# Fillers counted from TensorE's real idle time, a scheduler that tracks fetched instructions, and a new table of keys

## The chip, the cores and the metric

The kernel runs on one core of a Trainium2 chip. The number that counts is the device time of one execution in microseconds (us), as the median of several runs. TensorE (PE) does matrix products, VectorE (DVE), ScalarE (ACT) and GpSimd (POOL) do the element-wise work, and SyncE (SP) issues every transfer to and from the main memory. PE is in-order as seen here: a product that waits holds up all that is written behind it.

## The reference

Eight batches of eight heads, 576 positions, head size 64. Attention with two masks is followed by a gated block whose gate mixes positions:

```python
scores = scale * np.matmul(q, k.transpose(0, 1, 3, 2))
mask_local = (rel >= 0) & (rel < 32)
mask_strided = (rel >= 0) & (pos[None, :] % 32 == pos[:, None] % 32)
# heads 0..3 local, heads 4..7 strided; softmax; times v  -> x (8, 576, 512)
h = np.maximum(x @ w_in, 0.0)
u, v = h[..., :512], h[..., 512:]
v_n = (v - mean(v)) / np.sqrt(var(v) + 1e-06)
v_s = np.einsum('ts,bsd->btd', w_spatial, v_n) + b_spatial[None, :, None]
out = (u * v_s) @ w_out
```

`w_in` and `w_out` arrive as 64-bit floats, the rest as 32-bit floats.

## The kernel before

**The work.** A unit `t` of attention is a batch and a pair of heads; of the four units of a batch two are local and two strided. A unit loads q, k and v, computes scores (`f_s`: L412 local, 36 products; L522 strided, 32 products), masks and normalises them, transposes them on VectorE (L465, L572), copies them into `ptl` or `pts` on ScalarE and GpSimd (L342, L344), multiplies by v (`f_v`: L494 local, 6 products in each of two halves; L589 strided, 32 products), and rounds the result into a high and a low part (`x`, L364 and L352). These products use small pieces of the array and are called tiled.

The dense products are written as three products of high and low parts each. Per batch: `v` (L780, 16 groups of three, plus a tail tile), whose result passes `chain` (L742 to L767: relu, mean and variance, a power on GpSimd, the scaling) into `vn`; `u` (L822); `spatial` (L902, closed by two tail products L914 and L915, times `u` in L924); and `project` (L944), stored as `outT`. Each 64-bit weight tile is loaded raw (`weight`, staged in `vn`, `u` and `g`), converted by four VectorE or ScalarE steps (L654 to L676), and split into high (L342 or L344) and low part (L352).

An f32 product of the tiled kinds and of the fillers shows as two matmul records in the profile: 10 fillers in the order are x20 in the trace.

**What sets the order.** Nothing is written in the order in which it runs. `Program.add` collects operations with a key (a due time), the engines that may do them with a cost in ns, and what they read and write. `Program.order` then walks forward in modelled time, takes for the engine that is free first the ready operation with the smallest key, and fixes each engine's whole instruction list. `KEYS` shifts the keys: `a` for the first eight units of attention, `v` and `u` for the tiles of `w_in`, `o` for `w_out`, `s` and `t` for the spatial weights. When a dense operation comes up while PE is in tiled mode, `order` may put a ready tiled one with a key less than `near` later ahead of it.

**Fillers.** `emit` walks the fixed order again. Where PE would be idle by the model for over `WARM_GAP` before an operation with a `spare` region, it puts products with a tile of zeros (L1066) into that region, which the real product overwrites. Their number is the modelled gap divided by `WARM_COST` (double in the first 4 us). Operations with a spare are the scores, the products with v, and the first product of a `v` tile.

**Transfers.** SP issues all loads in one in-order list, so a load that waits for a buffer holds up those behind it. q, k and v have two buffers each. `cst`, the masks (L994), has the key -200. Score tiles `s` are a ring of two: a unit's scores wait until the masks of the tile that lay there before have been applied (L432, L537).

Of the kernel before, what the change touches and what calls it, by code (L numbers as in the profile page):

```python
# [21 lines left out]
P = 128  # L22
STRIDE = 32
# [9 lines left out]
SB = STRIDE // 4  # L33
# [5 lines left out]
KEYS = {  # L39
    "a": (-1894.0, -126.2, -779.7, -79.4, 376.7, -12.1, -10.1, 227.1,),  # L40
    "v": (-128.3, -81.4, -413.7, -1231.9,),
    "u": (-53.3, 26.9, 4.7, -65.3,),
    "s": (531.9, 556.2, 1682.3, 644.7,),
    "o": (302.1, 188.1, 252.3, 1053.5,),
    "t": (1077.7,),
    "lead": (2.85,),
    "dp": (1925,),
    "dpt": (159.07,),
    "fill": (-733.8, 1585.7, 207.5, -196.5, 2223.1, 42.9,),
    "near": (149.92,),  # L50
}
WARM_END, WARM_GAP, WARM_SLACK, WARM_COST = 110000.0, 300.0, 100.0, 165.0
DMA_RATE = 275.0
# [4 lines left out]
PE, ACT, DVE, POOL, DMA = "tensor", "scalar", "vector", "gpsimd", "sync"  # L58
# [67 lines left out]
class Program:  # L126
# [3 lines left out]
    def __init__(self):  # L130
        self.ops, self.writer, self.readers, self.spare = [], {}, {}, {}
        self.tiled, self.port = set(), {}

    def add(self, key, choices, fn, reads=(), writes=(), spare=None, tiled=False, port=()):

        n = len(self.ops)
# [4 lines left out]
        if tiled:  # L141
            self.tiled.add(n)
        deps = set()
# [19 lines left out]
    def order(self):  # L163
# [10 lines left out]
        taken = [False] * len(ops)  # L174
        mode = False
        issued = []
# [24 lines left out]
        while len(issued) < len(ops):  # L201
# [19 lines left out]
            n = heapq.heappop(ready[e])[1]  # L221
            if e == PE and mode and n not in self.tiled:
                near = [
                    op for op in ready[PE]
                    if op[1] in self.tiled and op[0] < ops[n][0] + KEYS["near"][0]
                ]
                if near:
                    heapq.heappush(ready[PE], (ops[n][0], n))
                    ready[PE].remove(min(near))
                    heapq.heapify(ready[PE])  # L230
                    n = min(near)[1]
# [30 lines left out]

    def emit(self, nc, warm):


        ends, free = {}, 0.0
        for at, n, e in self.order():
# [18 lines left out]
def attention_moe(ctx, tc, qT, kT, vl, vs, cst, w_in, w_out, wsp, wtail, out):  # L286
# [115 lines left out]
    def local_attention(t, due, q, kl, v, kin):  # L402
# [4 lines left out]
        def f_s(eng):  # L407
# [15 lines left out]
            due - 14, [(PE, 26 * 2 * S // STRIDE)], f_s, [(q,), *kin], [(p,) for p in s_ps],  # L423
            spare=(s_ps[0], lambda: s_ps[0]()[:32, :96]), tiled=True,
        )
# [61 lines left out]
        for c0 in (0, 3):  # L487
# [3 lines left out]
            def f_v(eng, c0=c0, o_ps=o_ps):  # L491
# [9 lines left out]
                due - 1.5, [(PE, 6 * 98)], f_v, [(v,), *ptok], [(o_ps,)],  # L501
                spare=(o_ps, lambda o_ps=o_ps: o_ps()[:32, :64]), tiled=True,
            )
# [5 lines left out]
    def strided_attention(t, due, q, k, v, kin):  # L509
# [8 lines left out]
        def f_s(eng):  # L518
# [13 lines left out]
            due - 14, [(PE, SB * 98)], f_s, [(q,), *kin], [(s_ps,)],  # L532
            spare=(s_ps, lambda: s_ps()[:32, :96]), tiled=True,
        )
# [49 lines left out]
        def f_v(eng):  # L584
# [12 lines left out]
        add(  # L597
            due - 1.5, [(PE, 4 * SB * 27)], f_v,
            [(v,), *(("pts", i) for i in range(4))], [(p,) for p in o_ps],
            spare=(o_ps[0], lambda: o_ps[0]()[:32, :64]), tiled=True,  # L600
        )
# [172 lines left out]
    def v_tile(key, step, x_at, m, toks):  # L774
        v_ps = r_pm.new()
        for kt in range(NT):

            def f(eng, kt=kt):
# [11 lines left out]
                toks(kt) + [("w_in", 1, kt, 0), ("w_in", 1, kt, 1)], [(v_ps,)],  # L790
                spare=None if kt else (v_ps, lambda v_ps=v_ps: v_ps()[:32, :128]),
            )
# [200 lines left out]

    add(-200, [(DMA, 330)], lambda eng: eng.dma_start(cst_sb, cst), (), [("cst",)])  # L994

# [66 lines left out]

    def warm(region, count):
        for _ in range(count):
            o = region()
            nc.tensor.matmul(  # L1066
                o, zeros, zeros[:, None, :].to_broadcast([P, o.shape[-1] // 32, 32]),
                start=True, stop=True,
            )
# [73 lines left out]
```

## Time and profile before

| | |
|---|---|
| median of three runs | 556.89 us (555.7 to 556.96) |
| the profiled execution's own time | 560.0 us |
| its span, first to last instruction | 557.7 us |
| PE busy (share of the span) | 526.0 us (94%) |
| DVE, ACT, POOL busy | 319.4, 234.1, 145.2 us |
| mean granted PE clock | 0.963 of full |
| transfers | 52.66 MB, 94 GB/s over the span |

All times in the prediction are on the span's axis, which starts at the first instruction. A row of a timeline gives start, duration (us), engine, line, operation, output<-input, shapes, count, and in brackets the idle time before it and what ended it; "issue" there means that nothing the profile shows was waited for. Records of one engine overlap by some 0.1 us, so a group's duration is from its first start to its last end. PEclk is the granted clock as a share of full speed.

### The profile page before, as it was taken

How to read it: one execution, taken by the hardware profiler on the slowest of the kernel's cores; microseconds unless marked ns; L12 is line 12 of the kernel's file. 1: busy time of each engine (PE TensorE's matmuls, PEld its weight loads, DVE VectorE, ACT ScalarE, POOL GpSimd, SP SyncE). 2: the span in 40 equal slices, each digit the busy share in tenths (PEclk: the TensorE clock that was granted, in tenths of full speed). 3: DMA queues.
4: the chain of work that ended last, by engine and by line, in shares of the span. 5: the costliest groups of instructions: out<-in, count | busy, mean ns of one | idle time of the engine just before them, and what ended most of it. 6: DMA issues, size and time to landing. Idle time of an engine off the chain costs nothing.

```text
span 557.7 us, 15920 instructions
## 1 busy us (share of the span) xinstructions
PE 526.0 (94%) x6608; PEld 486.5 (87%) x6608; DVE 319.4 (57%) x1010; ACT 234.1 (42%) x747; POOL 145.2 (26%) x235
## 2 busy tenths in 40 slices
PE   3687897999999999999999998999999999999997
PEld 2565795998989989999999987999899989998997
DVE  2856897725545377852974576862884462535232
ACT  3746655755665445331641444341642132313211
POOL 3544778645546132100310021200410010001000
PEclk8579887999999999999999999999999999999999
DMA  8735582315235232231251322231121200010011
GB/s 260 242 125 205 145 316 75 105 64 161 87 104 164 86 110 85 74 125 44 75 154 45 115 85 73 80 105 44 51 69 42 71 12 2 21 43 23 1 42 43
DMA packets 26103, 52.66 MB, mean 94 GB/s; under 512 B 3120, under 2 KB 11440, under 8 KB 26032
## 3 DMA queue, kind: packets, MB, share of 16 engines
q1 hardware_dynamic: 26032, 51.65, 29.1%
q8 instruction: 52, 0.85, 0.7%
q14 instruction: 19, 0.16, 0.1%
HBM read 42.21 MB, written 9.44 MB: 93 GB/s over the span
## 4 chain that ended last, share of the span: by engine, by line
PE 90%; DVE 3%; issue 2%; DMA 2%; SPq 1%; POOL 1%; ACT 1%; ACTq 0%; DVEq 0%
PE m L780 19%; PE m L944 19%; PE m L902 18%; PE m L822 17%; PE po L494 4%; PE po L589 3%; PE s L412 2%; PE s L522 2%; PE m L914 2%; DMA vn<-w_in 2%; PE m L915 2%; PE m L1066 1%; PE po L1066 1%; SPq L371 1%; PE s L1066 0%
## 5 line engine op out<-in xcount | busy, mean ns | idle before, releaser
L902 PE MATMUL m<-wsp_sb,vn 128*128 128x288 f32 x768 | 110.9, 295 | 0.0
L822 PE MATMUL m<-x,w_in_sb 128*128 128x288 f32 x768 | 108.0, 300 | 2.5 <-POOL w_in_sb L352 1.8
L822 PEld LDWEIGHTS m<-x,w_in_sb 128*128 128x128 f32 x768 | 105.2, 191 | 4.6 <-POOL w_in_sb L352 2.0
L944 PE MATMUL m<-g,w_out_sb 128*128 128x288 f32 x768 | 106.2, 297 | 0.0
L902 PEld LDWEIGHTS m<-wsp_sb,vn 128*128 128x128 f32 x768 | 105.3, 189 | 0.7
L944 PEld LDWEIGHTS m<-g,w_out_sb 128*128 128x128 f32 x768 | 103.4, 188 | 0.6
L780 PE MATMUL m<-w_in_sb,x 128*128 128x512 f32 (+1 forms) x408 | 103.3, 408 | 0.0
L780 PEld LDWEIGHTS m<-w_in_sb,x 128*128 128x128 f32 (+1 forms) x408 | 75.8, 190 | 20.4 <-issue 2.4
L760 POOL TENSOR_TENSOR bn<-bn,sel 128x1 f32<-128x1 f32 (+1 forms) x37 | 21.3, 576 | 215.4 <-DVE bn L755 212.4
L924 DVE TENSOR_TENSOR u<-m,u 128x288 f32<-128x288 f32 x64 | 28.3, 455 | 72.8 <-PE m L915 72.6
L364 ACT COPY o<-m 128x288 f32<-128x288 f32 x59 | 23.5, 399 | 104.6 <-PE m L944 91.8
L449 ACT ACTIVATE pl<-pl,ml 128x64 f32<-128x64 f32 (+1 forms) x160 | 53.6, 338 | 5.3 <-DVE ml L432 5.2
L747 DVE BATCH_NORM_STATS2 bn<-vv 128x6 f32<-128x512 f32 (+1 forms) x37 | 25.5, 689 | 53.0 <-ACT vv L742 52.8
L344 POOL TENSOR_SCALAR ptl<-pc 32x320 f32<-32x320 f32 (+3 forms) x80 | 31.6, 395 | 53.6 <-PE po L494 39.2
L836 ACT ACTIVATE u<-m 128x288 f32<-128x288 f32 x64 | 25.6, 408 | 38.2 <-PE m L822 36.5
L742 ACT ACTIVATE vv<-m 128x512 f32<-128x512 f32 (+1 forms) x37 | 22.1, 596 | 46.3 <-PE m L780 45.6
L364 ACT CAST x<-po 128x288 fp32r<-128x288 f32 x54 | 20.3, 399 | 50.0 <-PE po L494 25.7
L352 DVE TENSOR_TENSOR x<-po,x 128x288 fp32r<-128x288 f32 x64 | 27.2, 451 | 21.8 <-ACT x L364 21.4
L522 PE MATMUL s<-kbd,q 128*32 128x36 f32 x1024 | 13.3, 206 | 18.8 <-DVE ml L432 12.4
L767 DVE TENSOR_SCALAR vv<-vv,bn 128x512 f32<-128x512 f32 (+1 forms) x37 | 22.6, 614 | 14.0 <-POOL bn L760 13.9
L449 ACT ACTIVATION_READ_ACCUMULATOR pl<-pl,ml 128x1 f32 (+1 forms) x160 | 30.3, 189 | 0.0
L522 PEld LDWEIGHTS s<-kbd,q 128*32 128x32 f32 x1024 | 11.6, 115 | 20.5 <-issue 20.0
(116 smaller groups left out, 659.2 us busy)
## 6 DMA issues: line engine op xcount, KB each, us to landing
q<-qT SPq DMA_DIRECT2D x32, 295.0 KB, 4.4
outT<-o SPq DMA_DIRECT2D x64, 144.0 KB, 1.8
v_raw<-vs SPq DMA_DIRECT2D x16, 512.0 KB, 3.8
v_raw<-vl SPq DMA_DIRECT2D x16, 384.0 KB, 3.8
k<-kT SPq DMA_DIRECT2D x16, 304.0 KB, 4.6
kbd<-kT SPq DMA_DIRECT2D x32, 144.0 KB, 4.4
vn<-w_in SPq DMA_DIRECT2D x4, 512.0 KB, 7.6
x<-wsp SPq DMA_DIRECT2D x4, 288.0 KB, 5.7
```

The lines of the kernel that those rows point to most:

```text
L344: eng.tensor_scalar(dst(), src(), 1.0, 0.0, op0=ALU.mult, op1=ALU.add)
L352: eng.tensor_tensor(dst(), src(), f32(hi()), op=ALU.subtract)
L364: eng.copy(dst(), src())
L449: eng.activation(p_sb()[:m, u, :], p_sb()[:m, u, :], AF.Exp, bias=st()[:m, u : u + 1], scale=-1.0, accum_out=st()[:m, NU + u : NU + u + 1],)
L522: eng.matmul(s_ps()[STRIDE * i : STRIDE * i + STRIDE, 2 * RA * c : 2 * RA * (c + 1)].rearrange("p (j k) -> p j k", j=2), q()[:, r : r + ST ...
L747: lambda eng: eng.bn_stats(bn()[:m, 0:6], v()[:m]), [(v,)], [(bn,)],
L780: eng.matmul(v_ps()[:m, :], x_at(kt)[:, a, :], w_in_sb[:, w, kt, HF:], start=(kt == 0 and i == 0), stop=(kt == NT - 1 and i == 2),)
L822: eng.matmul(u_ps()[:, :HS], w_in_sb[:, w, kt, f * P : (f + 1) * P], xs[NHP * b + kt]()[:, a, r], start=(kt == 0 and i == 0), stop=(kt == ...
L836: lambda eng, u=u, f=f, u_ps=u_ps: eng.activation(u()[:, f * HS : (f + 1) * HS], u_ps()[:, :HS], AF.Relu),
L902: eng.matmul(s_ps()[:, :HS], vn()[:, a, kt, fs], wsp_sb[:, w, kt, r], start=(kt == 0 and i == 0), stop=False,)
L924: lambda eng, ug=ug, s_ps=s_ps: eng.tensor_tensor(ug(), s_ps()[:, :HS], ug(), op=ALU.mult),
L944: eng.matmul(o_ps()[:, :HS], w_out_sb[:, w, f, e * P : (e + 1) * P], g[a]()[:, f, :], start=(f == 0 and i == 0), stop=(f == NT - 1 and i = ...
```

## The change

Five edits go together.

1. Fillers: 256 columns wide in place of 64, 96 or 128; counted as half (`WARM_SHARE`) of the modelled gap divided by 427 ns, for gaps over 800 ns, and no longer ahead of `v` tiles in the order that results. The gap starts at `free`, the modelled end of PE's last operation. Before, where an operation had fillers, its own cost was overwritten by that of one filler before `free` was taken (the line `cost = WARM_COST ...`), so the next gap counted from too early; now the operation's own cost stands. By the orders, 74 fillers become 20.
2. The model of PE now keeps a stock of fetched products: it refills by one in 32 ns up to 200, each operation takes a number from it (72, 64 or 12 for the tiled ones, which is their count of records in the profile, 3 for others), and a shortfall costs 32 ns each. A tiled operation that is larger than the stock gives way to a ready dense one, and one may be put forward only if it is smaller than the stock.
3. Two costs in the model are raised: GpSimd's rounding copy (L344) and the strided product with v.
4. `cst` gets a key of its own, -952.3.
5. All keys are new. The sequence of the first eight units stays the same; among the weights, the second `u` tile (`u` entry 1) moves from eighth to third.

The diff, cut to its core:

```diff
 KEYS = {
-    "a": (-1894.0, -126.2, -779.7, -79.4, 376.7, -12.1, -10.1, 227.1,),
-    "v": (-128.3, -81.4, -413.7, -1231.9,),
-    "u": (-53.3, 26.9, 4.7, -65.3,),
-    "s": (531.9, 556.2, 1682.3, 644.7,),
...
+    "a": (-2171.5, -625.6, -893.2, -356.9, 1325.6, -222.2, -52.3, 22.3,),
+    "v": (-407.2, -245.7, -878.2, -1404.4,),
+    "u": (-86.3, -477.1, 14.3, -106.1,),
+    "s": (434.1, 1240.4, 3115.7, 449.8,),
...
+    "cst": (-952.3,),
+    "near": (280.07,),
 }
-WARM_END, WARM_GAP, WARM_SLACK, WARM_COST = 110000.0, 300.0, 100.0, 165.0
+WARM_END, WARM_GAP, WARM_COST, WARM_COLS, WARM_SHARE = 110000.0, 800.0, 427.0, 256, 0.5
+FETCHED, FETCH_COST = 200.0, 32.0
...
-            if e == PE and mode and n not in self.tiled:
-                near = [
-                    op for op in ready[PE]
-                    if op[1] in self.tiled and op[0] < ops[n][0] + KEYS["near"][0]
-                ]
-                if near:
+            if e == PE:
+                stock = min(FETCHED, stock + (now - since) / FETCH_COST)
+                since = now
+                other = []
+                if n in self.tiled:
+                    if self.tiled[n] > stock:
+                        other = [op for op in ready[PE] if op[1] not in self.tiled]
+                elif mode:
+                    other = [
+                        op for op in ready[PE]
+                        if self.tiled.get(op[1], FETCHED) < stock
+                        and op[0] < ops[n][0] + KEYS["near"][0]
+                    ]
+                if other:
...
                 mode = n in self.tiled
+                stock -= self.tiled.get(n, 3)
+                cost += FETCH_COST * max(0.0, -stock)
...
-                if n in self.spare:
-                    buf, region = self.spare[n]
-                    since = max([free, 600.0, *(ends[m] + 200.0 for m in buf.before)])
-                    if at - since > WARM_GAP and at < WARM_END:
-                        cost = WARM_COST if since > 4000.0 else 2.0 * WARM_COST
-                        warm(region, int((at - since - WARM_SLACK) / cost))
+                if n in self.spare and at < WARM_END:
+                    before = self.spare[n][0].before
+                    gap = at - max([free, 600.0, *(ends[m] + 200.0 for m in before)])
+                    if gap > WARM_GAP:
+                        found[n] = int(WARM_SHARE * gap / WARM_COST)
...
-        cost = {ACT: 95 + 0.833 * n, DVE: 70 + 0.52 * n, POOL: 110 + 0.95 * n}
+        cost = {ACT: 95 + 0.833 * n, DVE: 70 + 0.52 * n, POOL: 110 + 1.1 * n}
...
-            due - 1.5, [(PE, 4 * SB * 27)], f_v,
+            due - 1.5, [(PE, 4 * SB * 34)], f_v,
...
-    add(-200, [(DMA, 330)], lambda eng: eng.dma_start(cst_sb, cst), (), [("cst",)])
+    add(KEYS["cst"][0], [(DMA, 330)], lambda eng: eng.dma_start(cst_sb, cst), (), [("cst",)])
...
-    def warm(region, count):
+    def warm(buf, count):
         for _ in range(count):
-            o = region()
             nc.tensor.matmul(
-                o, zeros, zeros[:, None, :].to_broadcast([P, o.shape[-1] // 32, 32]),
+                buf()[:STRIDE, :WARM_COLS], zeros,
+                zeros[:, None, :].to_broadcast([P, WARM_COLS // STRIDE, STRIDE]),
                 start=True, stop=True,
             )
```

Lines of the changed kernel are 20 further down than those of the kernel before in the functions that matter here (L780 becomes L800, L432 becomes L452, L1066 becomes L1085). Three places show how the change moves instructions. The first is SP's list of loads at the start; q, k, `v_raw` and `kbd` (strided keys) belong to units of attention, `vn` is the staging tile of the first raw weights. Before:

```order
L371 DMA v_raw_117<-vl 128x768
L371 DMA vn_122<-w_in 128x1024
L371 DMA q_172<-qT 128x590
L371 DMA kbd<-kT 64x576 x2
L371 DMA v_raw_178<-vs 128x1024
L371 DMA vn_122<-w_in 128x1024
L994 DMA cst_sb<-cst 128x192
```

Now, from the same place:

```order
L391 DMA v_raw_117<-vl 128x768
L391 DMA vn_122<-w_in 128x1024
L1014 DMA cst_sb<-cst 128x192
L391 DMA q_167<-qT 128x590
L391 DMA kbd<-kT 64x576 x2
L391 DMA v_raw_175<-vs 128x1024
L391 DMA vn_122<-w_in 128x1024
```

The masks' load has moved ahead of one q, two halves of k, one v and the second weight tile. VectorE's list follows: the masking of the first scores (L452) now comes straight after the first step on the first weight tile, where before three more steps on weights stood between.

The second place is PE around the first products with v (`ptl`, tiles `po_388` and `po_414` before, `po_323` and `po_339` now) and the first `v` tile. Before:

```order
L522 MATMUL s_325<-kbd,q_247 32x36 x32
L1066 MATMUL po_388<-zeros 32x64 x16
L494 MATMUL po_388<-ptl,v_raw_117 64x96 x6
L1066 MATMUL po_414<-zeros 32x64
L494 MATMUL po_414<-ptl,v_raw_117 64x96 x6
L1066 MATMUL m_448<-zeros 32x128 x12
L780 MATMUL m_448<-w_in_sb,x_430 128x512 x3
L1066 MATMUL po_468<-zeros 32x64 x2
```

Now:

```order
L1085 MATMUL po_323<-zeros 32x256
L514 MATMUL po_323<-ptl,v_raw_117 64x96 x6
L514 MATMUL po_339<-ptl,v_raw_117 64x96 x6
L1085 MATMUL s_370<-zeros 32x256 x2
L542 MATMUL s_370<-kbd,q_312 32x36 x32
```

The 16 and the 12 fillers are gone, one of the new kind stands there, and the strided scores that stood ahead of the products with v come behind them. The first `v` products come later, behind the next local scores.

The third place is PE at those `v` products (`m_…` are their tiles) and the second local unit's product with v (`po_600`, `po_618` before, `po_571`, `po_582` now). Before:

```order
L1066 MATMUL m_555<-zeros 32x128 x4
L780 MATMUL m_555<-w_in_sb,x_430 128x512 x3
L1066 MATMUL m_570<-zeros 32x128 x2
L780 MATMUL m_570<-w_in_sb,x_430 128x512 x3
L1066 MATMUL m_581<-zeros 32x128 x2
L780 MATMUL m_581<-w_in_sb,x_430 128x512 x3
L1066 MATMUL po_600<-zeros 32x64 x7
L494 MATMUL po_600<-ptl,v_raw_438 64x96 x6
L1066 MATMUL po_618<-zeros 32x64 x2
L494 MATMUL po_618<-ptl,v_raw_438 64x96 x6
```

Now:

```order
L800 MATMUL m_533<-w_in_sb,x_354 128x512 x3
L800 MATMUL m_543<-w_in_sb,x_354 128x512 x3
L800 MATMUL m_558<-w_in_sb,x_354 128x512 x3
L514 MATMUL po_571<-ptl,v_raw_356 64x96 x6
L514 MATMUL po_582<-ptl,v_raw_356 64x96 x6
L800 MATMUL m_592<-w_in_sb,x_354 128x512 x3
L1085 MATMUL s_610<-zeros 32x256
L542 MATMUL s_610<-kbd,q_548 32x36 x32
```

The `v` products stand side by side with no fillers between, and one filler in place of 17 is left in this stretch.

More of the change, by code (lines that the diff above doesn't have):

```diff
@@ L131, in __init__, with add @@
         self.ops, self.writer, self.readers, self.spare = [], {}, {}, {}
-        self.tiled, self.port = set(), {}
-    def add(self, key, choices, fn, reads=(), writes=(), spare=None, tiled=False, port=()):
+        self.tiled, self.port = {}, {}
+    def add(self, key, choices, fn, reads=(), writes=(), spare=None, tiled=0, port=()):
         n = len(self.ops)
@@ L141, in add @@
         if tiled:
-            self.tiled.add(n)
+            self.tiled[n] = tiled
         deps = set()
@@ L174, in order @@
         taken = [False] * len(ops)
-        mode = False
+        mode, stock, since = False, FETCHED, 0.0
         issued = []
@@ L221, in order @@
             n = heapq.heappop(ready[e])[1]
-            if e == PE and mode and n not in self.tiled:
-                near = [
-                    op for op in ready[PE]
-                    if op[1] in self.tiled and op[0] < ops[n][0] + KEYS["near"][0]
-                ]
-                if near:
+            if e == PE:
[12 more added lines that the diff above has]
+                if other:
                     heapq.heappush(ready[PE], (ops[n][0], n))
-                    ready[PE].remove(min(near))
+                    ready[PE].remove(min(other))
                     heapq.heapify(ready[PE])
-                    n = min(near)[1]
+                    n = min(other)[1]
             cost = dict(ops[n][1])[e]
@@ L261, in order, with fillers @@
         return sorted(issued)
-    def emit(self, nc, warm):
-        ends, free = {}, 0.0
-        for at, n, e in self.order():
+    def fillers(self, issued):
+        ends, free, found = {}, 0.0, {}
+        for at, n, e in issued:
             cost = dict(self.ops[n][1])[e]
@@ L270, in emit @@
             if e == PE:
-                if n in self.spare:
-                    buf, region = self.spare[n]
-                    since = max([free, 600.0, *(ends[m] + 200.0 for m in buf.before)])
-                    if at - since > WARM_GAP and at < WARM_END:
-                        cost = WARM_COST if since > 4000.0 else 2.0 * WARM_COST
-                        warm(region, int((at - since - WARM_SLACK) / cost))
-                free = at + cost
+                if n in self.spare and at < WARM_END:
[3 more added lines that the diff above has]
+                        found[n] = int(WARM_SHARE * gap / WARM_COST)
+                free = at + cost
+        return found
+    def emit(self, nc, warm):
+        issued = self.order()
+        fillers = self.fillers(issued)
+        for _, n, e in issued:
+            if e == PE and fillers.get(n):
+                warm(self.spare[n][1], fillers[n])
             self.ops[n][2](getattr(nc, e))
@@ L423, in local_attention @@
             due - 14, [(PE, 26 * 2 * S // STRIDE)], f_s, [(q,), *kin], [(p,) for p in s_ps],
-            spare=(s_ps[0], lambda: s_ps[0]()[:32, :96]), tiled=True,
+            spare=(s_ps[0], s_ps[0]), tiled=72,
         )
@@ L501, in local_attention @@
                 due - 1.5, [(PE, 6 * 98)], f_v, [(v,), *ptok], [(o_ps,)],
-                spare=(o_ps, lambda o_ps=o_ps: o_ps()[:32, :64]), tiled=True,
+                spare=(o_ps, o_ps), tiled=12,
             )
@@ L532, in strided_attention @@
             due - 14, [(PE, SB * 98)], f_s, [(q,), *kin], [(s_ps,)],
-            spare=(s_ps, lambda: s_ps()[:32, :96]), tiled=True,
+            spare=(s_ps, s_ps), tiled=64,
         )
```

17 lines of the change are left out of this document (8 added, 9 removed).

## The prediction

> **What bounds the kernel now.** I read the busy times first, then the stretches, then PE's waits, then the start engine by engine.
>
> ```profile
> PE 526.0 (94%) x6608; PEld 486.5 (87%) x6608; DVE 319.4 (57%) x1010; ACT 234.1 (42%) x747; POOL 145.2 (26%) x235
> ```
>
> ```profile
> core 0: us, PE busy (x) PEld busy (x) DVE busy (x) ACT busy (x) POOL busy (x), PEclk, DMA share, GB/s
> 0.00:20.00 20.00, 7.95 (x196) 7.22 (x201) 8.27 (x34) 9.40 (x28) 6.54 (x17) 0.72 0.78 242
> 20.00:40.00 20.00, 15.63 (x324) 12.83 (x305) 12.12 (x44) 10.11 (x37) 12.31 (x20) 0.68 0.56 172
> 40.00:60.00 20.00, 16.39 (x273) 12.01 (x253) 14.15 (x45) 11.86 (x40) 8.37 (x8) 0.92 0.59 197
> 60.00:80.00 20.00, 18.19 (x238) 16.58 (x237) 18.38 (x38) 12.62 (x28) 15.36 (x18) 0.91 0.76 252
> 80.00:100.00 20.00, 17.12 (x219) 14.41 (x218) 15.94 (x43) 11.75 (x39) 16.41 (x16) 0.83 0.27 91
> ```
>
> PE is the bound, but in the first 100 us it is busy for only 75.3, and not all of that is work:
>
> ```profile
> sum 558.00, PE 20.23 PEld 15.92; mean PE 2.02 PEld 1.59
> ```
>
> That is the sum over the span for L1066 alone: 20.2 us are fillers. From 60 to 80 DVE is at 92%, so a front that comes sooner meets DVE next. PE's longest waits:
>
> ```profile
> PE s L522 <- DVE ml L432: 12.4, 2, 10.8
> PE s L522 <- issue: 6.4, 3, 3.4
> ```
>
> Idle time in sum is 557.7 - 526.0 = 31.7 us. So up to 52 us are not work, and nearly all of it lies in the start. What the change can win is there.
>
> **1. The masks' load (`cst`) earlier.** The 10.8 us are the wait of the first strided scores, which need a score tile back from the masks.
>
> ```profile
> 6.19 0.66 SPq L994 DMA_DIRECT2D cst_sb<-cst  x1
> ...
> DMA to landing us min/median/max: 8.8/8.8/8.8
> ...
> 9.88 0.43 DVE L661 TENSOR_SCALAR vn<-vn 128x512 int32<-128x512 int32 x1 [7.51 <-DMA vn<-w_in]
> ...
> 14.72 0.43 DVE L661 TENSOR_SCALAR vn<-vn 128x512 int32<-128x512 int32 x1 [2.70 <-DMA vn<-w_in]
> 15.08 0.23 DVE L432 CUSTOM_DVE_ANT_0 pl<-s,cst_sb 128x64 f32<-128x64 f32 x1
> ...
> 16.66 1.19 PE L522 MATMUL s<-kbd,q 128*32 128x36 f32 x64 [10.84 <-DVE ml L432]
> ```
>
> ```profile
> q<-qT SPq DMA_DIRECT2D x32, 295.0 KB, 4.4
> ...
> v_raw<-vs SPq DMA_DIRECT2D x16, 512.0 KB, 3.8
> ...
> kbd<-kT SPq DMA_DIRECT2D x32, 144.0 KB, 4.4
> vn<-w_in SPq DMA_DIRECT2D x4, 512.0 KB, 7.6
> ```
>
> `cst` landed at 6.19 + 8.8 = 15.0, and the masks began at once. Between the landings of the two `vn` tiles (9.88 and 14.72) came 295 + 2 x 144 + 512 + 512 = 1607 KB, 332 KB per us. Now `cst` (96 KB) stands behind the first `vn` and lands at 9.88 + 0.3 = 10.2; q and two `kbd` follow by 583/332 = 1.8 us, at 12.0. The ten masks took 15.08 to 16.6, so they end near 11.8, and the scores start at 12.0 in place of 16.66: **-4.6**. Lower bound of the gain 0.3 (if the second `vn`, which still lands at about 15, were what the chain waits for; VectorE has all masks written ahead of it, so I take the whole), upper 4.9 (15.08 to 10.2). The loads that `cst` is moved past come 0.3 us later, inside these numbers.
>
> **2. Fillers that overrun their gap.**
>
> ```profile
> 32.03 4.79 PE L1066 MATMUL m<-zeros 128*32 128x128 f32 x24
> ...
> 32.58 0.46 DVE L352 TENSOR_TENSOR x<-po,x 128x288 fp32r<-128x288 f32 x1 [0.98 <-ACT x L364]
> ...
> 36.76 0.96 PE L780 MATMUL m<-w_in_sb,x 128*128 128x512 f32 x3
> ```
>
> ```profile
> 40.25 2.22 ACT L342 COPY ptl<-pc 32x320 f32<-32x320 f32 x6
> ...
> 40.57 1.06 PE L1066 MATMUL m<-zeros 128*32 128x128 f32 x8
> ...
> 42.45 0.62 PE L1066 MATMUL m<-zeros 128*32 128x128 f32 x4
> 43.89 0.62 PE L1066 MATMUL m<-zeros 128*32 128x128 f32 x4
> 45.34 0.97 PE L1066 MATMUL po<-zeros 128*32 128x64 f32 x14
> 46.24 0.72 PE L494 MATMUL po<-ptl,v_raw 128*64 128x96 f32 x12
> ```
>
> The first `v` products had their last input at 32.58 + 0.46 = 33.04 and started at 36.76, 3.5 us after a start at 33.3. The products with v at 46.24 had `ptl` at 40.25 + 2.22 = 42.5; the four fills ahead of them take 1.06 + 0.62 + 0.62 + 0.97 = 3.3, the work between them 3 x 0.96, so without fills they start at 40.6 + 2.9 = 43.5: 2.7 us. Together **-6.2**.
>
> What replaces them: 12 fillers of 128 columns in 4.79 us are 0.40 each, in a stretch of half clock (below), so one of 256 columns is an estimated 0.80 there and 0.40 to 0.62 at full clock (two of 128 took 0.62 at 42.45). The six ahead of the second local scores last 4.8 us after 13.2, until 18; by the rate above that unit's k lands at about 17, and its masks stand on VectorE behind the first unit's transposition, which covers the last us. The six ahead of the third local scores stand behind a k that SP issues after a v load, which itself waits for a strided product; a v lands 3.8 us after its issue and the k after it, so cover is 4 to 5. The first four (3.2 us) end before the first q lands (4.4 after its issue). The other four (3.2 us) stand ahead of products whose inputs pass ScalarE and GpSimd first. I take 0; bounds 0 and +3.2 for those four, so the term lies between -3 and -8 (the latter if the other old fills, 20.2 - 4.8 - 3.3 = 12.1 us, overran by 15% too).
>
> **3. Instruction fetch.**
>
> ```profile
> 30.17 0.42 PE L494 MATMUL po<-ptl,v_raw 128*64 128x96 f32 x1 [2.83 <-issue]
> ...
> 55.32 0.32 PE L522 MATMUL s<-kbd,q 128*32 128x36 f32 x12 [3.43 <-issue]
> 55.58 8.80 PE L780 MATMUL m<-w_in_sb,x 128*128 128x512 f32 x30
> ...
> 319.66 7.16 PE L780 MATMUL m<-w_in_sb,x 128*128 128x512 f32 x30
> ```
>
> ```profile
> q8 instruction: 52, 0.85, 0.7%
> ```
>
> Both stalls fall inside a group that had started, so no input was missing. PE has 6608 products and as many weight loads; 52 instruction packets make one per 127 products. The stalls therefore look like a block that had not arrived, in stretches of heavy loads (the first three 20-us rows show DMA at 0.56 to 0.78). The second also cooled PE: the 30 products behind it took 8.80 us against 7.16. Cost 2.83 + 3.43 + 1.64 = 7.9. The change spaces tiled groups in the model and has 108 fewer records, which shifts every block edge. It has no term for loads, so I give it half: **-4**, bounds -7.9 and +3.4 (one more stall).
>
> [...]
>
> Later stalls in L522 are 6.4 - 3.43 = 3.0. The run strided product, two strided scores, local product occurs five times in a row of groups in both orders, so I change nothing: 0, bounds -3 and +3.
>
> **4. Spatial weights.** One tile of `wsp` now gets its low part on VectorE behind the scaling of the first tail tile (L787), before `spatial` can finish.
>
> ```profile
> 90.57 4.62 PE L780 MATMUL m<-w_in_sb,x 128*64 128x512 f32 x12
> 95.03 6.48 PE L902 MATMUL m<-wsp_sb,vn 128*128 128x288 f32 x48
> ...
> 97.97 1.51 DVE L767 TENSOR_SCALAR vv<-vv,bn 64x512 f32<-64x512 f32 x1 [0.17 <-POOL bn L760]
> ```
>
> The tail tile ended at 95.2 and was scaled by 99.5, 4.3 later; a low part (one element-wise step of that size, 1.5 by the same row) follows: 5.8. PE has 24 spatial products (half of 6.48, 3.2), a strided product of 64 records (1.19 by the row at 16.66, less at full clock) and local scores of 72 ahead, some 5. **+1**, bounds 0 and +3.
>
> Edits 3 and the keys otherwise only move work that lies beside PE; the amounts per engine are unchanged.
>
> **The sum and what VectorE allows.** -4.6 - 6.2 - 4 + 1 = -13.8. But VectorE must do the same steps before each PE group. Its setup is over before 4 us:
>
> ```profile
> 0.00:4.00 4.00, 3.06 (x20) 3.06 (x20) 1.25 (x5) 3.27 (x4) 3.30 (x14) 1.00 0.53 162
> ```
>
> Its first data come at 9.88; from there to 60 us it was busy 8.27 - 1.25 + 12.12 + 14.15 = 33.3 of 50.1 us. In 60 to 100, where it is pressed, its share is (18.38 + 15.94)/40 = 0.86. At that share 33.3 us take 38.8, and it comes forward by 11.3 us; at the 0.92 of 60 to 80 by 13.9. I take the first, since three engines hand work to each other in this stretch: **-11.3**. Against the span, 557.7 - 11.3 = 546.4. The profiled execution's own time is 560.0; the median of the runs, 556.89, lies 0.8 under the span. From the median, **545.6 us**.
>
> **The rivals.**
>
> *VectorE keeps pace at 0.92 and no stall is left.* For it: masks no longer queue behind weight steps. Against: GpSimd and VectorE slow each other when both are dense. -13.9 and up to -3 later: 540 to 543.
>
> *Only the masks' gain survives.* Late landings of v and q hold the next units where they were: SP's list is in order, and a v load waits for a product. -2 to -7: 550 to 555.
>
> *The front is lost again by 95 us.* `spatial` needs all the weight tiles; if VectorE's idle 16.8 us move elsewhere in place of going, it starts where it did: within 0.3%, which is about what a measurement of this kernel can tell from no change.
>
> *Slower: PE stays at half clock.* Fillers drop from 20.2 us to at most 20 x 0.80 = 16, and by count half the gap at full clock.
>
> ```profile
> 32.00:36.00 4.00, 4.00 (x21) 3.23 (x20) 3.31 (x5) 2.25 (x5) 2.34 (x2) 0.50 0.62 208
> 36.00:40.00 4.00, 4.00 (x118) 3.07 (x116) 0.39 (x2) 0.82 (x3) 2.07 (x6) 0.98 0.16 43
> ```
>
> Here full clock came after 4 us without a gap, which were mostly fillers, and each us of full-rate work costs one more at half. From 60 to 100 PE was busy 18.19 + 17.12 us; if over 11.3 us of that work run at half clock in their new place the gain is gone, at 15 the time is 561. That takes seven restarts at the 1.64 us of the one above. Against it: the clock from 60 to 80 was 0.91 although the 3.43 us stall had come shortly before.
>
> [...]
>
> **How the numbers follow.** Likeliest, 543 to 550: 0.50. Better than that: 0.17. Masks only: 0.13. Within 0.3%: 0.07. Slower: 0.13. Faster is 0.50 + 0.17 + 0.13 = 0.80. For 8 in 10, the range leaves out the slow case and the lowest edge: 537 to 556.
>
> **What would show it.** Right: first strided scores near 12 (term 1); no L1085 group directly ahead of a `v` product, and fewer than 16 us of L1085 (2); "issue" waits of PE under 7 us in all (3); the first spatial products near 84 rather than 95, with VectorE over 85% busy from 10 to 80 (sum). Wrong: PEclk at 0.5 between 45 and 80, new waits of PE on `w_in_sb` or on `ptl` in that stretch, or a new "issue" stall there.

## The result, and the profile after

The changed kernel takes 542.36 us (median of four runs, 539.54 to 543.93), the kernel before beside it 556.92 (555.70 to 557.15): a ratio of 0.9737, 95% interval 0.9691 to 0.9783. Forecast were 545.6, 537 to 556, and faster at 0.8. The profiled execution took 543.93 with a span of 542.1; that of before had 557.7, so the two traces differ by 15.6 us. In four later series the kernel before ran between 545.5 and 559.4 us (and once 831.93), most of the time near 551 or 555; a ratio leaves out runs more than 1.5% above the fastest, so differences of medians and ratios can differ by some us. The trace of before is of a long execution, 560.0 us, and there is one trace for each kernel: single traces show where time goes, and the medians of one series say how much.

Busy times after, and the first 100 us in five stretches (columns as in the prediction):

```profile
PE 515.1 (95%) x6500; PEld 471.4 (87%) x6500; DVE 323.9 (60%) x1026; ACT 235.5 (43%) x751; POOL 127.7 (24%) x215
```

```profile
0.00:20.00 20.00, 10.91 (x230) 5.82 (x230) 8.72 (x38) 9.91 (x30) 8.62 (x21) 0.83 0.87 267
20.00:40.00 20.00, 14.63 (x280) 9.38 (x278) 18.61 (x71) 16.38 (x59) 16.03 (x21) 0.91 0.79 225
40.00:60.00 20.00, 17.45 (x286) 14.70 (x287) 17.26 (x34) 12.55 (x35) 15.05 (x16) 1.00 0.82 254
60.00:80.00 20.00, 17.47 (x282) 14.50 (x281) 18.30 (x49) 14.59 (x43) 14.27 (x14) 0.91 0.55 187
80.00:100.00 20.00, 19.99 (x304) 19.25 (x297) 14.35 (x67) 17.00 (x70) 14.91 (x21) 1.00 0.43 133
```

DVE is now pressed from 20 us on (18.61, 17.26, 18.30 of 20), where before it had 12.12 and 14.15 in the second and third stretch. L1085 alone, over the span:

```profile
sum 543.00, PE 13.77 PEld 5.16; mean PE 13.77 PEld 5.16
```

So 13.8 us of fillers stand in place of 20.2. PE's waits, the longest first:

```profile
PE s L542 <- DMA kbd<-kT: 9.3, 2, 7.0
PE s L542 <- issue: 2.5, 2, 1.9
PE m L800 <- ACT u L856: 2.2, 1, 2.2
```

The 10.8 us for VectorE's masks are gone; the scores wait for the strided keys instead. The start (SP, VectorE, PE) and then PE up to the first `project` products, of which the last row has its counterpart of before beneath it:

```profile
2.57 0.43 SPq L1014 DMA_DIRECT2D cst_sb<-cst  x1
...
9.80 0.43 DVE L681 TENSOR_SCALAR vn<-vn 128x512 int32<-128x512 int32 x1 [7.43 <-DMA vn<-w_in]
10.28 0.22 DVE L452 CUSTOM_DVE_ANT_0 pl<-s,cst_sb 128x64 f32<-128x64 f32 x1
...
13.32 1.19 PE L542 MATMUL s<-kbd,q 128*32 128x36 f32 x64 [7.01 <-DMA kbd<-kT]
...
27.05 4.16 PE L1085 MATMUL s<-zeros 128*32 128x256 f32 x12
32.85 0.96 PE L432 MATMUL s<-k,q 64*32 64x64 f32 x72 [1.64 <-DMA k<-kT]
33.75 2.36 PE L800 MATMUL m<-w_in_sb,x 128*128 128x512 f32 x9
36.03 1.21 PE L514 MATMUL po<-ptl,v_raw 128*64 128x96 f32 x24
...
40.96 0.76 PE L542 MATMUL s<-kbd,q 128*32 128x36 f32 x64 [2.27 <-DMA kbd<-kT]
...
43.23 6.57 PE L800 MATMUL m<-w_in_sb,x 128*128 128x512 f32 x27
...
78.14 0.95 PE L922 MATMUL m<-wsp_sb,vn 128*128 128x288 f32 x6
...
90.13 6.69 PE L964 MATMUL m<-g,w_out_sb 128*128 128x288 f32 x48
```

```profile
106.88 6.69 PE L944 MATMUL m<-g,w_out_sb 128*128 128x288 f32 x48
```

At the first `project` product PE has done the same groups in both orders, so this row is the measure of the front in all that follows: 16.8 us sooner in these two traces. From there to the end it is 450.8 us before and 452.0 after. In the traces the change won in the front, all of it, and lost about 1 us behind it. How much an ordinary execution wins is less: one of 552 us with the same rest would start `project` near 99 (552 - 450.8, less the 2.3 us by which the profiled time exceeds its span; an estimate).

### The profile page after: what moved, and what is told of

Its sections match the earlier page's. It is cut to its first block, busy times and chain, and to the rows that moved or that the text cites. A ratio compares the mean times of both kernels' runs of the same rounds, so it can differ in the third digit from the quotient of the medians.

```text
span 542.1 us, 15698 instructions
## 1 busy us (share of the span) xinstructions
PE 515.1 (95%) x6500; PEld 471.4 (87%) x6500; DVE 323.9 (60%) x1026; ACT 235.5 (43%) x751; POOL 127.7 (24%) x215
## 4 chain that ended last, share of the span: by engine, by line
PE 83%; DVE 6%; DMA 4%; POOL 2%; issue 2%; SPq 1%; ACT 0%; POOLq 0%; ACTq 0%; DVEq 0%
PE m L964 19%; PE m L922 18%; PE m L800 17%; PE m L842 17%; PE po L609 3%; PE po L514 3%; DMA g<-w_in 2%; PE s L432 2%; PE m L934 2%; DMA kbd<-kT 2%; PE m L935 2%; PE s L542 2%; SPq L391 1%; POOL ptl L364 1%; DVE vv L787 1%
## 5 line engine op out<-in xcount | busy, mean ns | idle before, releaser
L800 PE MATMUL m<-w_in_sb,x 128*128 128x512 f32 (+1 forms) x408 | 100.9, 403 | 2.2 <-ACT u L856 2.2
L800 PEld LDWEIGHTS m<-w_in_sb,x 128*128 128x128 f32 (+1 forms) x408 | 74.8, 187 | 21.8 <-ACT u L856 2.4
L780 POOL TENSOR_TENSOR bn<-bn,sel 128x1 f32<-128x1 f32 (+1 forms) x37 | 21.4, 577 | 226.0 <-DVE bn L775 221.9
L767 DVE BATCH_NORM_STATS2 bn<-vv 128x6 f32<-128x512 f32 (+1 forms) x37 | 25.4, 687 | 42.0 <-ACT vv L762 41.9
L364 POOL TENSOR_SCALAR ptl<-pc 32x64 f32<-32x64 f32 (+3 forms) x83 | 32.9, 396 | 68.7 <-PE po L514 52.7
L362 ACT COPY ptl<-pc 32x64 f32<-32x64 f32 (+3 forms) x77 | 26.1, 339 | 6.9 <-DVE pc L485 3.9
L384 ACT CAST x<-po 128x288 fp32r<-128x288 f32 x49 | 18.5, 397 | 17.3 <-PE po L609 9.1
L372 DVE TENSOR_TENSOR g<-u,g 128x288 fp32r<-128x288 f32 x56 | 25.2, 460 | 1.1
```

Of the source, the lines that this page charges most:

```text
L362: eng.copy(dst(), src())
L364: eng.tensor_scalar(dst(), src(), 1.0, 0.0, op0=ALU.mult, op1=ALU.add)
L372: eng.tensor_tensor(dst(), src(), f32(hi()), op=ALU.subtract)
L384: eng.copy(dst(), src())
L800: eng.matmul(v_ps()[:m, :], x_at(kt)[:, a, :], w_in_sb[:, w, kt, HF:], start=(kt == 0 and i == 0), stop=(kt == NT - 1 and i == 2),)
```

## The experiments

This table has, beside the medians, two numbers of each profiled execution: the start of `project` (the front), and the time from there to the end of the span with the sum of PE's waits named "issue" of over 0.25 us in it.

| kernel | median us | ratio to before, 95% | project starts | rest of the span | issue waits in the rest |
|---|---|---|---|---|---|
| before | 552 to 557 | | 106.88 | 450.8 | 3.7 |
| after | 542.36 | 0.974 [0.969, 0.978] | 90.13 | 452.0 | 3.8 |
| a_again | 540.33 | 0.980 [0.976, 0.984] | 89.09 | 451.2 | 3.3 |
| b_cst5 | 555.89 | 1.005 [1.001, 1.008] | 103.33 | 448.6 | 2.4 |
| a_cst9 | 546.04 | 0.990 [0.986, 0.993] | 94.20 | 450.5 | 2.8 |
| b_newfill | 546.15 | 0.986 [0.980, 0.992] | 95.30 | 448.7 | 2.8 |
| b_nofill | 548.23 | 0.997 [0.994, 1.000] | 95.98 | 452.3 | 6.0 |
| b_shift | 548.04 | 0.989 [0.983, 0.995] | 97.53 | 450.5 | 2.3 |
| a_oldfill | 547.44 | 0.987 [0.978, 0.995] | 97.43 | 450.6 | 2.9 |
| a_nofill | 542.82 | 0.980 [0.974, 0.986] | 89.79 | 450.5 | 2.9 |
| a_narrow | 544.90 | 0.982 [0.976, 0.988] | 91.55 | 451.4 | 3.6 |
| c_k3 | 545.22 | 0.987 [0.981, 0.992] | 89.83 | 448.0 | 1.6 |
| c_front | 543.71 | 0.982 [0.978, 0.986] | 91.13 | 448.8 | 2.7 |
| c_front64 | 542.98 | 0.980 [0.976, 0.984] | 87.54 | 453.2 | 6.1 |

The names say the base: b for the kernel before, a for the changed one, c for further moves on the changed one. In some of them the lines stand a few further down. The changed kernel was run again beside `a_cst9`, `b_nofill` and `c_k3`, in one series with them:

> The changed kernel itself, once more, to stand beside the others of this series. Expected 540 to 544 us, and against the kernel before a ratio near 0.975 to 0.982. If the kernel before comes out near 551 in half of its runs again, as it did beside the first four experiments, the gain against those runs is 9 to 10 us and against the others (near 556) 14 to 15.

It came out at 540.33 (538.57 to 542.11, six runs), against 552.29 of before: 12.0 us, less than the 14.6 of the first series.

### The masks' load

`b_cst5` is the kernel before with SP's list alone changed.

```diff
+# SP's list only: the masks' load from 10th to 5th place
+moved = issued.pop(at)
+issued.insert(loads[3] + 1, moved)
```

> Before with the masks' load as fifth in SP's list in place of tenth, all else in its place (VectorE still has three weight steps ahead of the masks). Theory of the first term: masks at 12.0 (behind the weight steps that end there) in place of 15.1, first strided scores at 13.6, and 3 us of it kept to the end: 553 to 554.5. Rival, that the next landing of a weight tile (14.7, next in VectorE's list) holds the chain: 556 to 557.

Measured 555.89 against 552.07 of before in that series: not faster. (Its trace has `project` 3.6 us sooner than the long execution of before; the medians don't bear that out.) VectorE and PE at the start:

```profile
9.63 0.43 DVE L666 TENSOR_SCALAR vn<-vn 128x512 int32<-128x512 int32 x1 [7.26 <-DMA vn<-w_in]
...
15.28 0.43 DVE L666 TENSOR_SCALAR vn<-vn 128x512 int32<-128x512 int32 x1 [3.50 <-DMA vn<-w_in]
15.62 0.22 DVE L437 CUSTOM_DVE_ANT_0 pl<-s,cst_sb 128x64 f32<-128x64 f32 x1
...
17.20 1.19 PE L527 MATMUL s<-kbd,q 128*32 128x36 f32 x64 [11.38 <-DMA kbd<-kT]
```

The second weight tile's first step stands ahead of the masks in VectorE's list and waits for its load. The masks' data had landed at 10.1 us (issued at 2.58, 7.5 to landing) and lay there. `a_cst9` is the reverse: the order of the changed kernel, with the load put back behind the second weight tile.

```diff
+# SP's list only: the five loads behind it go ahead of the masks' load
+issued[at:at] = later
```

> The changed kernel with one move: the masks' load stands behind the second weight tile, as ninth of SP's loads, instead of fifth. VectorE's list keeps the masks straight behind the first weight step. Theory (the load and VectorE's place for the masks work only together, and the load then bounds the front): the load lands near 15, the masks start near 15, the first strided scores near 16.7 in place of 13.3, the first project product comes 3 to 4 us later, time 545 to 547. Rival (the front is bound by VectorE's later work, which has slack until 20 us to catch up): the scores are late by the same 3.4 us, but the first spatial products and project move by less than 1 us and the time stays at 541.5 to 543.5.

```profile
9.61 0.43 DVE L685 TENSOR_SCALAR vn<-vn 128x512 int32<-128x512 int32 x1 [7.23 <-DMA vn<-w_in]
15.14 0.23 DVE L456 CUSTOM_DVE_ANT_0 pl<-s,cst_sb 128x64 f32<-128x64 f32 x1 [5.11 <-DMA cst_sb<-cst]
...
16.73 1.19 PE L546 MATMUL s<-kbd,q 128*32 128x36 f32 x64 [10.83 <-DMA vn<-w_in]
```

Measured 546.04 against 540.33 of `a_again` in the same series: 5.7 us, and 5.1 at `project` (94.20 against 89.09). So the load is worth this where the masks also stand early in VectorE's list, and nothing where they don't. The early place alone, in the old order, was not run.

### The fillers

`b_newfill` has the order of before with the new fillers (10 of 256 columns in place of 74), `b_nofill` has none.

```diff
-                        warm(region, int((at - since - WARM_SLACK) / cost))
+                        pass
```

> The order of before, every instruction but the fillers in its place; the fillers alone by the new rule and width (10 of 256 columns in place of 74 narrow ones: 4, 1, 3 and 2 ahead of the first, second and fourth group and of the first v product). Theory that overrunning fillers were a term of their own: the 6.2 us of the prediction's second term go, less some clock lost in 36 to 50 us where nothing warms PE now: 550 to 553. Rival, that the order is what counted: 555 to 557, because the products then wait for VectorE in the same places.

> The kernel before without any fillers; order and everything else as before. Theory (the fillers only do harm where they overrun, and the clock they give is worth nothing while other engines bound the front): the same as the old order with the new, fewer fillers, 545 to 548 us, although the granted clock stays at half until some 35 us. Rival (fillers are worth their place through the clock, and only their number was too high): 550 to 556 us, with PE at half clock in stretches where it is busy throughout.

The new fillers in the old order gave 546.15, against 552.07 of before in that series: 5.9 us by medians, about half of the 12.0 that `a_again` won. Without any, `project` starts nearly as early (95.98 against 95.30), and the median, in another series, is 548.23, 4.1 below before (by the ratio, 0.997, hardly 2); behind `project` its waits named issue are 6.0 us in place of 2.8. So in the old order the old fillers had no value that these runs show, and taking them all out cost nothing.

`a_oldfill` puts the old rule and widths back into the changed order, `a_nofill` takes all fillers out of it, and `a_narrow` makes them 64 columns wide and four times as many.

```diff
-            if e == PE and fillers.get(n):
+            if False and e == PE and fillers.get(n):
```

> The order of after, with fillers counted and shaped as before (over 100 narrow ones, 35 and 38 of them ahead of the second and third local scores). Theory of overrunning fillers: 35 fillers of 96 columns last 35 x 0.34 = 12 us at half clock where some 4 us are free, and PE comes late twice: +8 to +12 over after, 550 to 555. Rival, that VectorE bounds the front whatever PE does: 542 to 545.

> The order of after with no filler at all. Theory that the fillers' worth is PE's clock (in the trace of after it is at full from 16 us on, before only from 36): PE runs at half clock until about 47, the 9 us of work it does in 14 to 43 become up to 14, part of it hidden behind VectorE: +2 to +5, 544 to 548. Rival, that the front is VectorE's alone: within 1 us of after, 541.5 to 543.5.

> The changed kernel with fillers of 64 columns in place of 256 and four times as many of them, 80 for 20; the same zeros into the same regions. Theory (what counts is that fillers end before the real work's inputs come; their width does not matter by itself): 540 to 544 us, as the changed kernel, with L1085 in sum at 11 to 16 us. Rival (the width is the point, since many short products use up PE's program and clock worse): 545 to 549, with stalls named issue of 2 us or more ahead of 60 us.

The old fillers in the new order cost 4.6 us against none by medians (547.44, 542.82, one series), half of the 8 to 12 expected. The two intervals of the ratios overlap, and the four runs of `a_oldfill` lie in two pairs, near 545 and near 550; its trace is of one near 550. First `a_oldfill`, where 70 records hold the second local scores until 20.85, then `a_nofill`, where these start at 16.91, when their k lands:

```profile
13.77 7.15 PE L1079 MATMUL s<-zeros 128*32 128x96 f32 x70
20.85 0.97 PE L425 MATMUL s<-k,q 64*32 64x64 f32 x72
```

```profile
16.91 1.32 PE L432 MATMUL s<-k,q 64*32 64x64 f32 x72 [2.72 <-DMA k<-kT]
...
33.44 1.32 PE L432 MATMUL s<-k,q 64*32 64x64 f32 x72 [6.08 <-DMA k<-kT]
34.69 4.21 PE L800 MATMUL m<-w_in_sb,x 128*128 128x512 f32 x9
...
42.77 6.93 PE L800 MATMUL m<-w_in_sb,x 128*128 128x512 f32 x27
```

`a_nofill` runs cold: nine `v` products take 4.21 us at 34.69, against 2.36 after. Yet it reaches the 27 products at 42.77 (43.23 after) and `project` at 89.79 (90.13), and its ratio to before is that of `a_again`, 0.980. Where the cold time went can be read: after the change PE waits 2.27 us for strided keys until 40.96, and in `a_nofill` the same scores start at 40.93 without a wait. In the new order the fillers, and the clock that they give, win nothing that these runs show, because PE is not what this part of the front waits for. `a_narrow` lies between the two theories: 544.90, in four runs 544.67, 545.13, 539.63 and 545.33. Its profile, of the run of 544.67, shows stalls in the front:

```profile
28.47 2.37 PE L1085 MATMUL s<-zeros 128*32 128x64 f32 x39 [1.80 <-issue]
...
36.53 0.98 PE L514 MATMUL po<-ptl,v_raw 128*64 128x96 f32 x18 [1.07 <-issue]
...
44.03 0.86 PE L609 MATMUL po<-pts,v_raw 64*64 64x36 f32 x31 [3.47 <-issue]
```

Its expectation that width alone decides nothing is not confirmed: 120 more records brought three stalls of instruction fetch, 6.3 us in all, into the front. `project` starts only 1.4 us later than in the changed kernel for it. That a wide filler warms better was neither needed nor shown.

### Instruction fetch

`b_shift` is the kernel before with 40 more records in time in which PE was idle.

```diff
+if not shifted:
+    shifted.append(n)
+    warm(lambda: region()[:, :32], 20)
```

> The kernel before with 20 more fillers of 32 columns (40 matmul records) ahead of the first scores, where PE is idle; everything behind them stands 40 records later in PE's program. In the kernel before, the waits named issue fall behind about 347, 724, 3005, 3893 and 4656 records, whose distances are 3, 18, 7 and 6 times 127. Theory (a stall is a block of 127 products and their weight loads that had not arrived): every stall that is left falls again behind 93 + n x 127 records counted from the start, within about 8, so at other work than before; the two stalls of the front need not occur, and the time lies between 543 and 557. Rival (the stall belongs to the group of products, by a wait that the profile does not name): the same groups stall, the first products with v near 30 us by 2 to 3 us and the third strided scores near 55 by 3 to 4, behind about 387 and 764 records, and the time stays within 1 us of the kernel before.

More fillers and nothing else, and the median was 548.04 against 553.86 of before in one series (ratio 0.989). Of the waits of before (6.4 and 2.8 us) these are left:

```profile
PE s L525 <- issue: 2.3, 2, 2.0
...
PE m L825 <- issue: 0.5, 2, 0.2
```

Neither the first products with v nor the third strided scores stalled, so the stall does not belong to the group. The longest of the stalls that are left, 1.96 and 0.38 us, fall behind 3894 and 4656 records, where before they fell behind 3893 and 4656: the same counts, though every product behind the first scores now stands 40 records later. This is 9 off 93 + n x 127, a little more than expected.

Two other readings bind the stall to instruction blocks. In all fourteen traces the 53 waits named issue of over 0.25 us stand at nearly the same place in a count by 127: 93 records behind a multiple of it at the start, drifting to 80 to 84 late in the program, and never elsewhere. In the changed kernel they fall, among others, behind 220, 597, 3765 and 4527 records, distances of 2.97, 24.9 and 6.00 times 127. And a packet of the instruction queue appears shortly ahead of the end of each: the row of the queues of before between 27.5 and 28.0, where PE went on at 30.17, and of `c_front` between 40.5 and 41.0, where it went on at 43.37:

```profile
q8 instruction: 1, 0.02, 11.0%
```

```profile
q8 instruction: 1, 0.02, 16.3%
```

All 35 stalls of over 1 us in the fourteen traces read like this: PE went on 1.8 to 3.0 us after the end of the half microsecond with the packet. Loads are not needed for it. `b_nofill` stalled 1.15 us until 400.82, and this is all that its queues moved between 396.5 and 399.5; loads set in only behind that:

```profile
DMA packets 1, 0.02 MB, mean 5 GB/s; under 512 B 0, under 2 KB 0, under 8 KB 0
...
q8 instruction: 1, 0.02, 2.1%
```

But the longest stalls, 2.8 to 3.5 us, all lie in the front, among heavy loads (the load queue took 87% of the 16 engines in the two microseconds ahead of the packet of 3.43 us in before). Whether loads lengthen a stall is not shown.

### What bounds the new front

`c_k3` has no fillers, and takes k and q of the third local unit ahead of a v load that waits.

```diff
+for at in (19, 21):
+    issued.insert(loads[17], issued.pop(loads[at]))
```

> The changed kernel without fillers and with two loads earlier: k and q of the third local unit are issued ahead of the v load that waits for the first product with v, at about 16 and 18 us in place of 24 and 28. Without that move PE stood idle 6.1 us until 33.4 for this k. Theory (VectorE's list bounds the front from here on: its masks of that unit come at 34.8, behind weight steps, whatever the scores do): the third local scores start at 27.5 to 28 in place of 33.4, the first v products at 30 to 34, but the first project product stays within 1 us of 89.8, and the time is within 1 us of the kernel without fillers, 541.8 to 543.8. Rival (the loads bound the front): project comes 3 to 5 us sooner and the time is 538 to 540.

```profile
27.13 1.34 PE L435 MATMUL s<-k,q 64*32 64x64 f32 x72
30.45 0.79 PE L803 MATMUL m<-w_in_sb,x 128*128 128x512 f32 x1 [1.99 <-ACT w_in_sb L365]
...
43.99 6.33 PE L803 MATMUL m<-w_in_sb,x 128*128 128x512 f32 x26 [2.03 <-issue]
```

The scores came 6.3 us sooner (33.44 to 27.13) and the `v` products 4.2, and `project` did not move (89.83, 89.79). That k was not the bound. But neither was VectorE alone: PE met the next stall of fetch. The median, 545.22, is no gain and outside what was expected; two runs lie at 539.3 and 539.5, four at 544.8 to 545.8, and the profile is of the first kind, so what made the four longer stays open.

`c_front` puts the first loads into the order of need and the weight steps behind the masks; `c_front64` adds 64 records of fillers in idle time.

```diff
+for n, behind in ((0, 30), (82, 0), (83, 82), (84, 83), (75, 84), (31, 75), (112, 32), (113, 112), (77, 51), (76, 40)):
+    # masks, q, keys, weight tile, v, q, k on SP; weight steps on VectorE and ScalarE
...
+if n in (32, 69):      # c_front64 only: first scores, first products with v
+    warm(self.spare[n][1], 16)
```

> The changed kernel without fillers and with the first loads in the order in which they are needed: q, k, masks, q and strided keys of the second unit, first weight tile, v, then q and k of the third unit; the first steps on the weight tile stand behind the masks on VectorE, and behind five exponentials on ScalarE. By 332 KB per us behind a k that lands at 4.5, the masks land near 5, the strided keys near 6.7, the first weight tile near 8.2 (9.7 before), the second near 14.5 (15.4). Theory (the first strided scores set the front, as the late masks' load showed: 3.8 us there were 5.1 at project): the scores start at 6.5 to 8 in place of 13, project starts at 82 to 86 in place of 89.8, time 534 to 539. Rival (once the masks are early the weight tiles bound the front, and these land hardly earlier): the scores start as early, but the first v products and project come less than 2 us sooner, and the time is 539 to 543.

```profile
8.03 1.19 PE L546 MATMUL s<-kbd,q 128*32 128x36 f32 x64 [2.07 <-DMA kbd<-kT]
...
38.77 0.76 PE L546 MATMUL s<-kbd,q 128*32 128x36 f32 x64 [1.59 <-DMA kbd<-kT]
39.46 1.17 PE L613 MATMUL po<-pts,v_raw 64*64 64x36 f32 x64
43.37 8.01 PE L804 MATMUL m<-w_in_sb,x 128*128 128x512 f32 x27 [2.74 <-issue]
```

The strided scores start 5 us sooner than in `a_nofill`, the products with v at 39.46 still 2.2 (41.63 there); then 128 short products in 1.9 us use up a block, PE stands 2.74 us, and the 27 products behind run cold. `project` starts at 91.13, later than the 82 to 86 of the theory and later than the rival had it too. Of the 5 us, 2.2 were left at 40 us, and the stall took these. Hence `c_front64`, which moves the block's edge:

> The kernel with the first loads in the order of need and no fillers, plus 32 fillers of 32 columns (64 matmul records) in PE's idle time: 16 ahead of the first scores, 16 ahead of the first products with v. Everything behind stands 64 records later. Without them PE stalled 2.74 us at 43.37, directly behind 64 strided scores and 64 strided products with v, and the 27 products behind the stall ran cold (8.01 us against 6.9). Theory (a block of 127 short products is used up sooner than the next block can be fetched; 64 records put the block's edge between the two groups, with long products in either block): no stall named issue above 1 us ahead of 80 us, the 27 products start near 40.7 and take 6.9 to 7.2, project starts at 86.5 to 88.5 in place of 91.1, time 538 to 541. Rival (the stall is the landing of something else at that time, or VectorE holds the front anyway): a wait of 2 us or more at 40 to 44 stays, or it goes and project still starts at 90 to 91.5; time 542 to 545.

```profile
40.84 1.17 PE L613 MATMUL po<-pts,v_raw 64*64 64x36 f32 x64
41.94 6.57 PE L804 MATMUL m<-w_in_sb,x 128*128 128x512 f32 x27
...
87.54 6.68 PE L968 MATMUL m<-g,w_out_sb 128*128 128x288 f32 x48
```

The stall is gone as expected and `project` starts 3.6 us sooner than in `c_front`, but only 2.3 sooner than in `a_nofill`, though the strided scores start 4.6 sooner (8.39): something else holds the rest of the front, and which engine it is was not tested. The time is no better, 542.98 for the 538 to 541 expected, against 543.71 of `c_front` in another series. The edges moved in the whole program:

```profile
PE po L518 <- issue: 4.2, 3, 1.6
...
PE s L546 <- issue: 1.9, 2, 1.5
```

These lie behind `project` (151, 207, 271 and 396 us), 6.1 us in all in place of 2.7, and the rest of the span takes 453.2 in place of 448.8. Over the table, the rest of the span rises by about 1 us with each us of its issue waits, with exceptions of up to 1.3 us: 448.0 at 1.6, 448.7 and 450.5 at 2.8, 452.0 at 3.8, 452.3 at 6.0, 453.2 at 6.1. None of the further kernels beats the changed one.

## Why the prediction was right, point by point

**The sum.** The terms gave -13.8, and the cut by what VectorE allows made it -11.3; medians gave -14.6 in the first series and -12.0 in the later one, traces -15.6. So the times do not decide on the cut of 2.5 us. The traces speak against its reason: VectorE's share from 10 to 60 us is 43.1 of 50, the 0.86 that I used, but as a limit it doesn't hold. First spatial products came at 78.14, not 84, and in `c_front64` VectorE was at 18.60, 18.65 and 18.49 of 20 us in the three stretches from 20 to 80, or 0.93. A share that an engine shows while it also waits is no ceiling. What stood against the rival at 0.92, that GpSimd and VectorE slow each other, the trace of before shows for some steps: VectorE's scaling of the tail tile (L767) took 1.51 us at 97.97, with GpSimd's L396 beside it, and 0.54 at 164.35, alone; GpSimd's L550 took 1.13 at 73.65, with VectorE's weight steps beside it, and 0.68 at 127.45, alone. VectorE's masks (L432) took 0.22 either way.

That the number came so near is in part luck. What was measured one by one is 5.7 for the masks and 5.9 for the fillers with the stalls, 11.6 together. The forecast had 4.6 for the first and 10.2 for the second, and then took off 2.5 for another reason. Beside these two, the rest of the new order shows no gain of its own: `a_cst9`, which has the new order and the new fillers without the early masks, and `b_newfill`, the old order with new fillers, came out at 546.04 and 546.15, in two series.

**Term 1, masks, -4.6.** Right in its mechanism, and measured at 5.7 by taking the early load back. At the scores themselves it was 3.3 in this trace (13.32 for 16.66): the masks were on time (10.28 for a forecast 10.2), but the strided keys landed at 13.3 in place of 12.0. I had taken the place in VectorE's list as part of the change, and `b_cst5` shows that in the old order the load alone gave nothing.

**Terms 2 and 3, fillers -6.2 and fetch -4.** Their sum came true in part and their split did not. With the old order the new fillers gave 5.9 us, and 40 *more* records gave 5.8: either edit removed the two early stalls (0.4 us of waits named issue are left ahead of `project` in one, none in the other) and shortened the cold stretch behind them (30 `v` products in 7.56 and 7.26 us, for 8.80). I had priced the overrun and the stalls apart, -6.2 and -4; together they measured about 6. Since a filler also counts in a block, they may be largely one effect; no run separates them. Of issue waits ahead of `project`, 6.3 us became 0.9 (0.60 and 0.27), those behind it 3.7 became 3.8: no change, as I had taken. At most blocks no such wait shows: only six of 51 instruction packets in the changed kernel's trace go with one of over 0.25 us. But single ones took 1.9 us there, and 3.4 in the kernel before.

My cause for the stalls, heavy loads, is not the whole one: `b_nofill` stalled 1.15 us with none beside the packet. What all stalls behind `project` have in common is a row of over 127 short products, with six long ones behind it at most. That is not enough by itself: each trace has eleven such rows there, and two to five of them stalled for over 0.25 us. In the front a shorter row was enough in some cases: the stall of 3.43 us before has six `v` products among the 127 ahead of it.

**Term 4, late low part, +1.** It ended at 83.4 on VectorE, and the spatial products from 80.99 on ran without a wait: 0, its lower bound.

**The clock.** A rival had PE stay at half clock. It did not (0.91, 1.00, 0.91 from 20 to 80). But the price that it put on each cold us was wrong as well: `a_nofill` was cold up to 39 us, where its first record of full clock stands, and lost nothing.

**The scheduler's stock.** With the new keys and costs, the instructions of all five engines come in the same order, row by row, with the old rule and no stock. That edit does nothing here; the order comes from the keys and the raised costs.

**What would show it.** Scores near 12: 13.32. No L1085 directly ahead of a `v` product, and under 16 us: none, 13.8. Issue under 7 us: 5.0. First spatial near 84: 78.14, further than forecast. Of the signs of failure (half clock from 45 to 80, waits on `w_in_sb` or `ptl` there, a new stall) the trace has only 3.4 us at half clock from 74.3 on.

## What to carry to other kernels

A load that comes earlier is worth something only if the engine that uses its data also has that work early in its list (here 5.7 us with the masks early, and no gain in `b_cst5`, 555.89 against 552.07, without); change both, and test each alone. Before filling idle time to keep a clock, run the kernel without the filling: here 20 us of fillers won nothing (548.23 without, 552.29 with, one series), and the cold clock cost nothing where PE was not the bound (`project` at 89.79 in `a_nofill`, 90.13 after). Count instructions as well as time: where the edge of a block falls into or just behind a row of short products, PE can stall, here by up to 2.3 us behind `project` and up to 3.5 in the front. Added instructions moved every such edge behind them (40 records in `b_shift`, 64 in `c_front64`), so a gain in one place can return as a loss in another.

## What the runs showed of the hardware

A stall of fetch needs no traffic of loads: with none beside its packet there was one of 1.15 us. Among heavy loads the longest was 3.5. Forty records in idle time moved the median by 5.8 us. That is as much as either large edit of this change, and in this kernel a difference of 1% between two orders may be block edges alone.

The clock column doesn't show a cold PE everywhere. In `c_front64` it is at full in this stretch, while nine `v` products in it took 4.01 us, against 2.36 for the same nine in the changed kernel. The first clock record of this trace stands at 36.3 us, and the column counts time without a record as full:

```profile
20.00:40.00 20.00, 12.80 (x260) 10.45 (x260) 18.60 (x72) 16.57 (x61) 15.50 (x21) 1.00 0.73 230
```

```profile
32.63 4.01 PE L804 MATMUL m<-w_in_sb,x 128*128 128x512 f32 x9
```

The duration of like products is the safer reading.
